# Leaving the row maximum out of a softmax under a bound taken from the gains, with a branch to the path that keeps it

## The chip, the cores and the metric

The kernel runs on one core of one Trainium2 chip. The metric is the device time of one execution in microseconds (us); lower is better. A core has five engines that run side by side and meet through semaphores: TensorE (PE in the profile, with its weight loads as PEld), VectorE (DVE), ScalarE (ACT), GpSimd (POOL) and SyncE (SP, which here only issues DMAs and DMA transposes). Matmuls read SBUF, the on-chip memory of 128 partitions, and write PSUM, eight banks of 128 x 512 f32.

## The reference

Attention over 8 batch rows, 12 heads, 448 positions and head size 64, and behind it a feed-forward layer with a token shift.

```python
def rmsnorm(x, g):
    return x / np.sqrt(np.mean(x * x, axis=-1, keepdims=True) + 1e-06) * g
q_n, k_n = rmsnorm(q, g_q), rmsnorm(k, g_k)
scores = np.matmul(q_n, k_n.transpose(0, 1, 3, 2)) / np.sqrt(64)
scores = scores - np.max(scores, axis=-1, keepdims=True)
attn = np.exp(scores)
attn = attn / (np.sum(attn, axis=-1, keepdims=True) + 1e-09)
x = heads_side_by_side(np.matmul(attn, v))        # 8 x 448 x 768
x_prev = x shifted by one position
xk = mu_k * x + (1 - mu_k) * x_prev
xr = mu_r * x + (1 - mu_r) * x_prev
k = np.maximum(xk @ w_k, 0)                       # w_k 768 x 1024
v = k * k @ w_v                                   # w_v 1024 x 768
r = 1 / (1 + np.exp(-(xr @ w_r)))                 # w_r 768 x 768
return r * v
```

All inputs are f32 but w_k, w_v and w_r, which are 64-bit floats. The maximum changes the value of no probability, it only keeps exp in range. After the normalisation a row of q_n has at most the length of the largest gain times 8, and a score is at most 64 times the largest |g_q g_k|/8. For the inputs that the reference draws, the largest |g_q g_k|/8 is 0.657.

## The kernel before

*Work and tiles.* Heads go in pairs (48) and quads (24, two pairs). For each quad q and k are loaded, normalised and transposed (`stats`, L602, `preps`), and seven score groups are made (`scores`, L777), 168 in all. A group is 128 rows of queries for two heads: two PSUM banks `sc` of 128 x 448 scores. `expo` (L814) takes each bank: VectorE writes the negative row maximum into the small tile `sums`, and ScalarE's exp takes it as its bias, writes the exponentials and sums them. That is 2 x 168 = 336 banks. `probs` (L826) then has VectorE scale the two sums and take their reciprocals. From there two ways lead to the transposed probabilities `pT`:

- The 21 groups of the first three quads (`probs_pe`, L859) hold f32 exponentials in a tile `nat` (or `xk`, memory lent until the first batch row needs it). GpSimd multiplies by the reciprocal, TensorE transposes into PSUM, and ScalarE or VectorE copies to `pT`, whichever has the lower planned clock (`pick`, L222).
- The other 147 groups keep exponentials in `sc`. `split` (L887) makes them two f16 tiles: ScalarE writes the rounded product with the reciprocal, VectorE the remainder, and SyncE issues a DMA transpose of both into `pT`. The scores of these quads are three f16 matmul passes, those of the first three one f32 pass.

`attends` (L895) multiplies `pT` by v into the bank `ot`; six pairs make one batch row. `mixk` (L927) makes xk as two f16 tiles; `moe` (L1076) multiplies xk by w_k, squares, and after that does xr by w_r and the squares by w_v, row by row, three f16 passes each, into two banks `mm`. The first batch row goes on to w_r and w_v only when all 20 weight tiles are done.

*Weights.* `weights` (L983) turns 64-bit floats into f32: 20 tiles of 128 columns, each in two halves of 3 x 128 or 4 x 128 elements per partition. GpSimd makes the low bits from byte 3 of each double, in place in `raw` (or `kk`, lent memory). ScalarE takes the high word as an f32, scales it by 2^-112 and writes it to a bank `mm`; its Prelu, with a negative slope of -2^32, turns the sign into an exponent bit. VectorE shifts that by 3, which puts the sign bit in its place, and ORs the low bits. `LOW_TILES` holds all 20 tiles, so the other branch there is never taken. `wsplit` (L1012) then scales a tile and splits it into two f16 tiles (wkh and wkl, wrh and wrl, wvh and wvl).

*Order.* Every step is a Python generator that yields operations. `Plan` (L214 on) holds a planned clock for each engine, prices an operation (`price`, L170), and always issues the one that can start first by these clocks, less a tenth of its priority in ns (`run`, L324). `emit` (L266) pins each engine's order to the order of issue. So the order of all five engines is fixed when the kernel is built, and one change of an operation or a price shifts the order of all that follow. Rings of buffers bound how far steps run ahead: five banks `sc`, two `mm`, one `ot`, four `nat`, two `raw`, two `wf`. The priority of weight work (`wprio`) rises with planned time past 10 us per finished tile. Nearly all operations are recorded under L272, the line in `emit`, so the profile is read by tile names.

Of the kernel before, what the change touches and what calls it, by code (L numbers as in the profile page):

```python
# [17 lines left out]
HD = 64  # L18
# [19 lines left out]
LOW_TILES = range(0, 20)  # L38
# [66 lines left out]
F64_NEG = -2.0 ** 32  # L105
# [315 lines left out]
def attn_moe_kernel(tc, q, k, v, g_q, g_k, mu_k, mu_r, w_k, w_v, w_r, out):  # L421
# [109 lines left out]
    def setup():  # L531
# [9 lines left out]
        yield V.tensor_reduce(out=gm[:, 0:1], in_=G, axis=AX.X, op=ALU.max, apply_absolute_value=True)  # L541
        yield V.tensor_scalar(out=gm[:, 0:1], in0=gm[:, 0:1], scalar1=TINY, scalar2=None, op0=ALU.max)
# [271 lines left out]
    def expo(gi, j, both, sums, D, tp):  # L814
        sp = both[j]
        if tp is not None:
            yield V.tensor_reduce(out=sums[:, j:j + 1], in_=sp[:, 0:S], axis=AX.X, op=ALU.max, negate=True)
            yield A.activation(out=tp.bitcast(F32).rearrange("p a c -> p (a c)")[:, j * S:(j + 1) * S], in_=sp[:, 0:S], func=AF.Exp, bias=sums[:, j:j + 1], accum_out=sums[:, 4 + 2 * j:5 + 2 * j])
# [4 lines left out]
        yield A.activation(out=sp[:, 0:S], in_=sp[:, 0:S], func=AF.Exp, bias=sums[:, j:j + 1], accum_out=both[0][:, S + j:S + j + 1])  # L823
        D[j] = True

    def probs(gi, both, sums, D, tp):  # L826
# [16 lines left out]
        yield V.tensor_scalar(out=r, in0=both[0][:, S:S + 2], scalar1=1e-9, scalar2=2.0 ** -15, op0=ALU.add, op1=ALU.mult)  # L843
        yield V.reciprocal(out=r, in_=r)
# [14 lines left out]
    def probs_pe(u, x, t0, sums, tp):  # L859
        r = sums[:, 8:11:2]  # L860
        yield V.tensor_scalar(out=r, in0=sums[:, 4:7:2], scalar1=1e-9, scalar2=2.0 ** -15, op0=ALU.add, op1=ALU.mult)
        yield V.reciprocal(out=r, in_=r)
# [120 lines left out]
    def weights():  # L983
        for nm, w, kt, c, ci in WT:
# [3 lines left out]
            for i in range(0, kt, hk):  # L988
# [7 lines left out]
                if ci in LOW_TILES:  # L996
# [197 lines left out]
```

## Time and profile before

| | |
|---|---|
| median of 3 runs | 1023.7 us (1022.6 to 1023.84) |
| the profiled execution, first to last instruction | 1022.8 us (its own time is given as this span alone) |
| TensorE busy | 933.2 us, 91% |
| VectorE busy | 789.3 us, 77% |
| ScalarE busy | 748.2 us, 73% |
| GpSimd busy | 691.6 us, 68% |
| mean granted TensorE clock | 0.968 |
| row maxima on VectorE | 336, 194.3 us, 614 ns each |
| f16 copies of probabilities on ScalarE | 294 (242 into `nat`, 52 into `natx`), 655 and 653 ns each |

In the profile a line of a group reads: line of the code, engine, operation, tiles written <- tiles read, shapes, count | busy us, mean ns of one | idle time of the engine just before them, and who ended it. `natx`, `dfx` and `kfx` are further buffers of `nat`, `df` and `kf`. A matmul's end is modelled and matmuls overlap, so a busy TensorE need not be at its peak. The chain of waits follows the work that ended last backwards from the end, step by step to what released it; "issue" in it is time with no cause in the profile. The slices divide the span in 40 parts, each digit the busy tenths of one.

### The profile page before, as it was taken

The numbers are of one execution on the slowest core, as the hardware profiler recorded it, in microseconds if no ns is written. First come the engines' busy times: TensorE is split into PE (matmuls) and PEld (weight loads), VectorE is DVE, ScalarE is ACT, GpSimd is POOL, SyncE is SP. The second block draws the span as 40 slices with busy tenths as digits, with TensorE's granted clock in tenths as the row PEclk, the third lists the DMA queues.
The fourth block names the chain that finished last, engine by engine and source line by source line (L and its number), as shares of the span: only waits on it lengthen the run. The fifth ranks groups of instructions, "written<-read, shape, count | busy, mean of one in ns | idle before, by whom it ended". The sixth has DMA issues, their size and how long they took to land.

```text
span 1022.8 us, 18968 instructions
## 1 busy us (share of the span) xinstructions
PE 933.2 (91%) x6166; PEld 489.2 (48%) x6166; DVE 789.3 (77%) x1967; ACT 748.2 (73%) x1755; POOL 691.6 (68%) x738
## 2 busy tenths in 40 slices
PE   1678778778999899999999999999999999999997
PEld 1344334344554455445555555455455554455564
DVE  5888868998989689878988798969887898785000
ACT  2666748988789688798888788888887887684211
POOL 2587678862688576896788467967795679629501
PEclk9779889978999999999999999999999999999999
DMA  8442348785885797777986889579768986662011
GB/s 200 121 118 74 104 126 173 181 182 112 188 188 125 150 188 155 171 165 173 185 165 113 179 180 190 127 163 193 157 126 179 183 181 139 135 124 54 1 32 31
DMA packets 447043, 146.62 MB, mean 143 GB/s; under 512 B 418784, under 2 KB 443360, under 8 KB 446944
## 3 DMA queue, kind: packets, MB, share of 16 engines
q1 hardware_dynamic: 427408, 127.42, 59.2%
q10 hardware_dynamic: 19536, 18.00, 6.1%
q8 instruction: 48, 0.79, 0.3%
q14 instruction: 51, 0.42, 0.1%
HBM read 50.40 MB, written 11.01 MB: 60 GB/s over the span
## 4 chain that ended last, share of the span: by engine, by line
PE 54%; DVE 18%; ACT 9%; POOL 7%; issue 6%; DMA 4%; SPq 1%; ACTq 0%; POOLq 0%; DVEq 0%
PE mm L272 37%; PE ot L272 9%; PE sc L272 8%; DVE sums L272 4%; DVE nat L272 3%; POOL xk L272 2%; ACT nat L272 2%; ACT sc L272 2%; DVE sst L272 2%; DVE df L272 2%; DMA pT<-nat 1%; DVE stm L272 1%; POOL nat L272 1%; SPq L272 1%; POOL qk L272 1%
## 5 line engine op out<-in xcount | busy, mean ns | idle before, releaser
L272 PE MATMUL mm<-wvh,kk 128*128 128x384 f16 x896 | 234.4, 327 | 0.0
L272 PE MATMUL mm<-xk,wkh 128*128 128x448 f16 x768 | 209.5, 355 | 5.9 <-ACT kf L272 4.2
L272 DVE TENSOR_REDUCE sums<-sc 128x1 f32<-128x448 f32 x336 | 194.3, 614 | 23.4 <-PE sc L272 23.0
L272 ACT ACTIVATE sc<-sc,sums 128x448 f32<-128x448 f32 x294 | 180.9, 617 | 36.9 <-DVE sums L272 33.1
L272 ACT ACTIVATE nat<-sc,sums 128x448 f16<-128x448 f32 (+1 forms) x274 | 167.2, 653 | 24.9 <-DVE sums L272 13.1
L272 PE MATMUL mm<-wrh,xr 128*128 128x384 f16 x672 | 179.9, 331 | 0.0
L272 DVE SCALAR_TENSOR_TENSOR nat<-sc,sums,nat 128x448 f16<-128x448 f32 x242 | 158.3, 675 | 28.0 <-ACT nat L272 27.5
L272 PEld LDWEIGHTS <-kk 128*128 128x128 f16 (+1 forms) x1362 | 129.2, 98 | 97.2 <-issue 17.0
L272 PE MATMUL sc<-stk 64*128 64x448 f16 (+3 forms) x1104 | 135.0, 386 | 12.8 <-DVE nat L272 4.2
L272 PE MATMUL mm<-wvl,kk 128*128 128x384 f16 x448 | 146.0, 326 | 0.0
L272 PE MATMUL mm<-xk,wkl 128*128 128x448 f16 x384 | 135.8, 354 | 0.0
L272 PEld LDWEIGHTS <-xr 128*128 128x128 f16 x1008 | 96.9, 99 | 75.2 <-issue 16.3
L272 PE MATMUL mm<-wrl,xr 128*128 128x384 f16 x336 | 111.3, 331 | 0.0
L272 PEld LDWEIGHTS <-wkh 128*128 128x128 f16 x768 | 72.2, 98 | 80.5 <-issue 19.8
L272 PE MATMUL ot<-pT,vh 128*64 128x448 f16 x672 | 101.0, 359 | 2.6 <-issue 1.3
L272 POOL TENSOR_TENSOR o<-o,bsc 128x384 f32<-128x384 f32 x48 | 42.9, 894 | 78.6 <-DVE o L272 53.9
L272 POOL TENSOR_TENSOR qk<-qk,ss 128x896 f32<-128x896 f32 x36 | 63.3, 1758 | 43.2 <-DVE ss L272 28.5
L272 DVE SCALAR_TENSOR_TENSOR o<-o,mm 128x384 f32<-128x384 f32 x56 | 30.6, 546 | 78.0 <-PE mm L272 49.9
L272 ACT ACTIVATE o<-mm,bsc 128x128 f32<-128x128 f32 x144 | 45.6, 386 | 45.6 <-PE mm L272 33.6
L272 DVE SCALAR_TENSOR_TENSOR df<-x,bsc,df 128x448 f32<-128x448 f32 x68 | 65.7, 978 | 10.5 <-POOL df L272 10.3
L272 PEld LDWEIGHTS <-stk 64*128 64x128 f16 x1008 | 35.7, 98 | 70.7 <-issue 48.9
L272 POOL TENSOR_TENSOR nat<-nat 128x448 f32<-128x448 f32 x41 | 47.5, 1157 | 29.9 <-ACT nat L272 29.2
(167 smaller groups left out, 1802.0 us busy)
## 6 DMA issues: line engine op xcount, KB each, us to landing
out_dram<-o SPq DMA_DIRECT2D x56, 192.0 KB, 2.9
qk<-in_k_dram SPq DMA_DIRECT2D x46, 224.0 KB, 3.8
qk<-in_q_dram SPq DMA_DIRECT2D x108, 64.0 KB, 2.5
vf<-in_v_dram SPq DMA_DIRECT2D x96, 64.0 KB, 2.6
raw<-in_moe_w_v_dram ACTq DMA_DIRECT2D x12, 512.0 KB, 4.6
vf<-in_v_dram SPq DMA_DIRECT2D x96, 48.0 KB, 2.5
raw<-in_moe_w_r_dram ACTq DMA_DIRECT2D x12, 384.0 KB, 3.3
kk<-in_moe_w_k_dram ACTq DMA_DIRECT2D x8, 384.0 KB, 4.5
```

The lines of the kernel that those rows point to most:

```text
L272: r = op.fn(op.kw["out"], op.kw["value"]) if op.fn.__name__ == "memset" else op.fn(**op.kw)
```

## The change

The kernel function gets two arguments, `safe` and `flag`. It is built twice into one program.

- With `safe=False` (the path that runs first) no row maximum is taken, and exp has no bias. The small addition of 1e-9 to the sum becomes a factor. `split` gives the f16 copy to ScalarE or VectorE, by `pick`.
- In `setup`, VectorE writes `flag` = 1 if the largest |g_q g_k|/8, which is there already, is at most 64/64 = 1.
- Behind the whole first path each engine loads the flag into a register. If it is 0, the second path (`safe=True`) computes everything again with the maximum, in the same output.
- In the weight conversion of both paths Prelu becomes Copy, and a new VectorE operation writes the sign, as byte 3 of the low word, from byte 7, after GpSimd has read and rewritten the low word. The branch that was never taken goes.

```diff
-LOW_TILES = range(0, 20)
-F64_NEG = -2.0 ** 32
+BOUND = 64.0
@@ setup
         yield V.tensor_reduce(out=gm[:, 0:1], in_=G, axis=AX.X, op=ALU.max, apply_absolute_value=True)
+        if flag is not None:
+            yield V.tensor_scalar(out=flag, in0=gm[0:1, 0:1], scalar1=BOUND / HD, scalar2=None, op0=ALU.is_le)
@@ expo
+        kw = {}
+        if safe:
+            yield V.tensor_reduce(out=sums[:, j:j + 1], in_=sp[:, 0:S], axis=AX.X, op=ALU.max, negate=True)
+            kw["bias"] = sums[:, j:j + 1]
         if tp is not None:
-            yield V.tensor_reduce(out=sums[:, j:j + 1], in_=sp[:, 0:S], axis=AX.X, op=ALU.max, negate=True)
-            yield A.activation(out=tp..., in_=sp[:, 0:S], func=AF.Exp, bias=sums[:, j:j + 1], accum_out=...)
+            yield A.activation(out=tp..., in_=sp[:, 0:S], func=AF.Exp, accum_out=..., **kw)
             banks["sc"].put(sp)
-            D[j] = True
-            return
-        yield V.tensor_reduce(out=sums[:, j:j + 1], in_=sp[:, 0:S], axis=AX.X, op=ALU.max, negate=True)
-        yield A.activation(out=sp[:, 0:S], in_=sp[:, 0:S], func=AF.Exp, bias=sums[:, j:j + 1], accum_out=...)
+        else:
+            yield A.activation(out=sp[:, 0:S], in_=sp[:, 0:S], func=AF.Exp, accum_out=..., **kw)
         D[j] = True
+
+    def recip(r, total):
+        if safe:
+            yield V.tensor_scalar(out=r, in0=total, scalar1=1e-9, scalar2=2.0 ** -15, op0=ALU.add, op1=ALU.mult)
+        else:
+            yield V.tensor_scalar(out=r, in0=total, scalar1=(1 + 1e-9) * 2.0 ** -15, scalar2=None, op0=ALU.mult)
+        yield V.reciprocal(out=r, in_=r)
@@ split
-        yield A.activation(out=ph[:, j], in_=sp[:, 0:S], func=AF.Copy, scale=r[:, j:j + 1])
+        if safe or plan.pick("ACT", "DVE") == "ACT":
+            yield A.activation(out=ph[:, j], in_=sp[:, 0:S], func=AF.Copy, scale=r[:, j:j + 1])
+        else:
+            yield V.tensor_scalar(out=ph[:, j], in0=sp[:, 0:S], scalar1=r[:, j:j + 1], scalar2=None, op0=ALU.mult)
@@ weights
-                if ci in LOW_TILES:
-                    yield G_.tensor_scalar(out=low, in0=<byte 3 of raw>, scalar1=-15.5, scalar2=2.0 ** -5, ...)
-                    yield A.activation(out=z, in_=top.bitcast(F32), func=AF.Prelu, scale=F64_EXP, alpha=F64_NEG)
-                    yield V.scalar_tensor_tensor(out=fi[...], in0=zi, scalar=3, in1=low, ...)
-                else:
-                    ...
+                r8 = raw.bitcast(mybir.dt.uint8)[:, 0:hk, :].rearrange("p i (n b) -> p i n b", b=8)
+                yield G_.tensor_scalar(out=low, in0=r8[:, :, :, 3], scalar1=-15.5, scalar2=2.0 ** -5, op0=ALU.add, op1=ALU.mult)
+                yield V.tensor_scalar(out=r8[:, :, :, 3], in0=r8[:, :, :, 7], scalar1=128.0, scalar2=128.0, op0=ALU.is_ge, op1=ALU.mult)
+                yield A.activation(out=z, in_=top.bitcast(F32), func=AF.Copy, scale=F64_EXP)
+                yield V.scalar_tensor_tensor(out=fi[:, i:i + hk, :], in0=zi, scalar=3, in1=low, op0=ALU.logical_shift_left, op1=ALU.bitwise_or)
@@ kernel
-        attn_moe_kernel(tc, *args)
+        with tc.tile_pool(name="path", bufs=1) as pool:
+            flag = pool.tile([1, 1], I32, name="bounded")
+            attn_moe_kernel(tc, *args, safe=False, flag=flag)
+            fine = nc.values_load(flag[0:1, 0:1], min_val=0, max_val=1)
+            with tc.If(fine < 1, preferred_fallthrough_block=False):
+                attn_moe_kernel(tc, *args, safe=True)
```

More of the change, by code (lines that the diff above doesn't have):

```diff
@@ L418, in rsqrt, with attn_moe_kernel @@
             yield V.scalar_tensor_tensor(out=y, in0=t, scalar=1.5, in1=y, op0=ALU.add, op1=ALU.mult)
-def attn_moe_kernel(tc, q, k, v, g_q, g_k, mu_k, mu_r, w_k, w_v, w_r, out):
+def attn_moe_kernel(tc, q, k, v, g_q, g_k, mu_k, mu_r, w_k, w_v, w_r, out, safe, flag=None):
     nc = tc.nc
@@ L815, in expo @@
         sp = both[j]
+        kw = {}
+        if safe:
+            yield V.tensor_reduce(out=sums[:, j:j + 1], in_=sp[:, 0:S], axis=AX.X, op=ALU.max, negate=True)
+            kw["bias"] = sums[:, j:j + 1]
         if tp is not None:
-            yield V.tensor_reduce(out=sums[:, j:j + 1], in_=sp[:, 0:S], axis=AX.X, op=ALU.max, negate=True)
-            yield A.activation(out=tp.bitcast(F32).rearrange("p a c -> p (a c)")[:, j * S:(j + 1) * S], in_=sp[:, 0:S], func=AF.Exp, bias=sums[:, j:j + 1], accum_out=sums[:, 4 + 2 * j:5 + 2 * j])
+            yield A.activation(out=tp.bitcast(F32).rearrange("p a c -> p (a c)")[:, j * S:(j + 1) * S], in_=sp[:, 0:S], func=AF.Exp, accum_out=sums[:, 4 + 2 * j:5 + 2 * j], **kw)
             banks["sc"].put(sp)
-            D[j] = True
-            return
-        yield V.tensor_reduce(out=sums[:, j:j + 1], in_=sp[:, 0:S], axis=AX.X, op=ALU.max, negate=True)
-        yield A.activation(out=sp[:, 0:S], in_=sp[:, 0:S], func=AF.Exp, bias=sums[:, j:j + 1], accum_out=both[0][:, S + j:S + j + 1])
+        else:
+            yield A.activation(out=sp[:, 0:S], in_=sp[:, 0:S], func=AF.Exp, accum_out=both[0][:, S + j:S + j + 1], **kw)
         D[j] = True
+    def recip(r, total):
[4 more added lines that the diff above has]
+        yield V.reciprocal(out=r, in_=r)
     def probs(gi, both, sums, D, tp):
@@ L842, in probs @@
         r = sums[:, 8:11:2]
-        yield V.tensor_scalar(out=r, in0=both[0][:, S:S + 2], scalar1=1e-9, scalar2=2.0 ** -15, op0=ALU.add, op1=ALU.mult)
-        yield V.reciprocal(out=r, in_=r)
+        yield from recip(r, both[0][:, S:S + 2])
         E = {}
@@ L860, in probs_pe @@
         r = sums[:, 8:11:2]
-        yield V.tensor_scalar(out=r, in0=sums[:, 4:7:2], scalar1=1e-9, scalar2=2.0 ** -15, op0=ALU.add, op1=ALU.mult)
-        yield V.reciprocal(out=r, in_=r)
+        yield from recip(r, sums[:, 4:7:2])
         tf = tp.bitcast(F32).rearrange("p a c -> p (a c)")
@@ L995, in weights @@
                 zi = z.bitcast(I32)
-                if ci in LOW_TILES:
-                    yield G_.tensor_scalar(out=low, in0=raw.bitcast(mybir.dt.uint8)[:, 0:hk, :].rearrange("p i (n b) -> p i n b", b=8)[:, :, :, 3], scalar1=-15.5, scalar2=2.0 ** -5, op0=ALU.add, op1=ALU.mult)
-                    yield A.activation(out=z, in_=top.bitcast(F32), func=AF.Prelu, scale=F64_EXP, alpha=F64_NEG)
-                    yield V.scalar_tensor_tensor(out=fi[:, i:i + hk, :], in0=zi, scalar=3, in1=low, op0=ALU.logical_shift_left, op1=ALU.bitwise_or)
-                else:
-                    yield A.activation(out=z, in_=top.bitcast(F32), func=AF.Prelu, scale=F64_EXP, alpha=F64_NEG)
-                    yield V.tensor_scalar(out=zi, in0=zi, scalar1=3, scalar2=None, op0=ALU.logical_shift_left)
-                    yield V.scalar_tensor_tensor(out=fi[:, i:i + hk, :], in0=low, scalar=29, in1=zi, op0=ALU.logical_shift_right, op1=ALU.bitwise_or)
+                r8 = raw.bitcast(mybir.dt.uint8)[:, 0:hk, :].rearrange("p i (n b) -> p i n b", b=8)
[3 more added lines that the diff above has]
+                yield V.scalar_tensor_tensor(out=fi[:, i:i + hk, :], in0=zi, scalar=3, in1=low, op0=ALU.logical_shift_left, op1=ALU.bitwise_or)
                 R["raw"].put(raw)
```

## The prediction

> **What bounds the kernel now.** I read the page first: busy times, then the forty slices.
>
> ```profile
> span 1022.8 us, 18968 instructions
> ...
> PE 933.2 (91%) x6166; PEld 489.2 (48%) x6166; DVE 789.3 (77%) x1967; ACT 748.2 (73%) x1755; POOL 691.6 (68%) x738
> ...
> PE   1678778778999899999999999999999999999997
> ...
> DVE  5888868998989689878988798969887898785000
> ```
>
> TensorE is full from the tenth slice (25.6 us each) to the last, and it is not full before. The feed-forward of the first batch row goes on to wr and wv as soon as the last weight tile is split; the timeline of TensorE has the first such matmul here (start us, us):
>
> ```profile
> 235.89 0.50 PE L272 MATMUL mm<-wrh,xr 128*128 128x384 f16 x1
> ```
>
> I cut the span just before it, at 235 us, and again at 925 us, where attention has ended and only the feed-forward of the last batch row is left. The table of these three stretches (length, then busy us and instruction count of PE, PEld, DVE, ACT, POOL; granted clock; DMA share; GB/s):
>
> ```profile
> 0.00:235.00 235.00, 159.54 (x930) 85.02 (x932) 192.53 (x516) 159.45 (x356) 161.20 (x202) 0.88 0.56 141
> 235.00:925.00 690.00, 681.60 (x4689) 351.40 (x4687) 581.03 (x1431) 565.94 (x1346) 491.12 (x493) 0.99 0.77 162
> 925.00:1022.80 97.80, 92.08 (x552) 52.73 (x550) 15.76 (x21) 22.79 (x53) 39.33 (x44) 1.00 0.08 21
> ```
>
> In the opening TensorE is idle for 235 - 159.5 = 75.5 us. In the middle it is idle for 690 - 681.6 = 8.4 us, although VectorE is 84% busy there. In the end VectorE is nearly empty. So VectorE's work has a price in the opening and hardly any after it: **whatever is freed after 235 us can give back 8.4 us at most.** The opening's total is what is to be argued. There VectorE is the fullest engine, 192.5 of 235 = 82%; ScalarE and GpSimd have 68 and 69%. The chain of waits, cut to the opening, by engine and tile:
>
> ```profile
> by line: PE sc L272 10.6%; issue 10.5%; PE ot L272 9.8%; DVE sums L272 8.5%; DVE nat L272 4.2%; DMA xk<-in_q_dram 3.5%; POOL xk L272 3.4%; DVE sst L272 2.9%; DMA pT<-nat 2.9%; POOL nat L272 2.7%; ACT nat L272 2.6%; DMA raw<-in_moe_w_k_dram
> ```
>
> No engine owns it: VectorE's writes of `sums` (maximum, sum scaling, reciprocal) hold 8.5%, that is 20.0 us. Last, whom TensorE and ScalarE waited for in the opening (us in total, times, longest):
>
> ```profile
> PE sc L272 <- DVE nat L272: 24.0, 6, 21.2
> ```
>
> ```profile
> ACT stk L272 <- PE sc L272: 12.3, 8, 3.3
> ACT pT L272 <- PE sc L272: 11.1, 11, 3.6
> ACT x L272 <- PE ot L272: 8.6, 4, 3.9
> ACT nat L272 <- DVE sums L272: 8.2, 6, 3.8
> ...
> ACT xk L272 <- DVE sums L272: 4.8, 3, 1.9
> ```
>
> The wait of 21.2 us is the start (first loads and first normalisation), which the change doesn't touch. ScalarE's exp waited 8.2 + 4.8 = 13.0 us for maxima.
>
> **The change part by part.** *The maxima go.* VectorE's groups in the opening (count | busy us, mean ns | idle before):
>
> ```profile
> L272 DVE TENSOR_REDUCE sums<-sc 128x1 f32<-128x448 f32 x72 | 42.3, 615 | 5.8 <-PE sc L272 5.7
> ...
> L272 DVE TENSOR_SCALAR sums<-sums 128x2 f32<-128x2 f32 x21 | 8.6, 426 | 1.2 <-ACT nat L272 1.1
> ...
> L272 DVE RECIPROCAL sums<-sums 128x2 f32<-128x2 f32 x35 | 5.0, 156 | 0.2
> ...
> L272 DVE TENSOR_SCALAR sums<-sc 128x2 f32<-128x2 f32 x14 | 2.0, 150 | 0.1
> ```
>
> 72 of the 336 reductions lie there: 42.3 us off VectorE. Of the 57.9 us that write `sums` they are 73%, so 14.6 of the chain's 20.0 us, or 35% of their own busy time. The other 264 lie under a full TensorE.
>
> *Byte instructions come.* Each of the 20 weight tiles is converted in two halves. GpSimd's instruction on the low word stays, and each half gains one VectorE `tensor_scalar` which reads byte 7 and writes byte 3 of the same words, both in SBUF: 40 of them, 28 with 384 elements and 12 with 512. All lie in the opening, as the view of the tile `raw` shows (minimum, median and longest ns, first and last start in us):
>
> ```profile
> L272 POOL TENSOR_SCALAR raw<-raw x32: 527/553/964, 15.6 to 222.0; 128x384 int32<-128x384 uint8 x20, 128x512 int32<-128x512 uint8 x12
> ```
>
> The other 8 halves, of 384 elements, are in memory borrowed from `kk`. No row shows this instruction. The nearest rows are VectorE's `tensor_scalar` of these lengths (from PSUM), and its slowest small one between SBUF tiles:
>
> ```profile
> L272 DVE TENSOR_SCALAR muu<-muu 128x12 f32<-128x12 f32 x1 | 1.6, 1620 | 0.0
> ...
> L272 DVE TENSOR_SCALAR stk<-sc,gc 128x384 f32<-128x384 f32 x2 | 1.2, 614 | 1.0 <-PE sc L272 1.0
> ...
> L272 DVE TENSOR_SCALAR stk<-sc,gc 128x512 f32<-128x512 f32 x1 | 0.8, 752 | 0.2 <-PE sc L272 0.2
> ```
>
> I take 614 and 752 ns: 28 x 0.614 + 12 x 0.752 = 26.2 us. The low end is the row of 150 ns (two elements), 6.0 us; the high end the row of 1620 ns, 64.8 us. That last row shows a danger: twelve elements cannot need 1620 ns, so the instruction stood waiting for something. The scaling of sums shows it again, 426 ns between SBUF tiles against 150 ns from PSUM, 0.276 us more for the same two elements. With that wait on each byte instruction the 40 cost 37.2 us.
>
> The Trainium skill, SBUF — State Buffer, section "Who interferes with whom", has a reason: VectorE and GpSimd share one SBUF port pair, a `tensor_scalar` in a two-port mode wants it, and the loser "fully blocks" until the other instruction ends. The rows of 426 and 1620 ns agree. By the rule the byte instruction, which starts when GpSimd's own conversion ends and GpSimd's next instruction begins, would wait more often than not; the sum would then go by 37.2 us instead of 26.2, and the opening would gain 3.0 us instead of 9.4.
>
> Net on VectorE in the opening: -42.3 + 26.2 = -16.1 us. How much of it reaches the end lies between the chain's share of such work, 0.35 (5.6 us), and VectorE's busy share, 0.82 (13.2 us); neither is nearer, so the mean 0.585: **-9.4 us.** Behind a byte instruction on VectorE stand the OR of the same half and then the attention work; the OR is late by 0.65 us. Halves follow each other (222.0 - 15.6)/39 = 5.3 us apart and two raw buffers are there, so the longer chain is covered; without that cover it is 40 x 0.655 = 26.2 us once more.
>
> *Copies may move.* In the opening ScalarE writes 28 f16 copies of probabilities:
>
> ```profile
> L272 ACT ACTIVATE nat<-sc,sums 128x448 f16<-128x448 f32 x28 | 17.1, 642 | 2.5 <-DMA pT<-nat 1.7 <-DVE sums L272 0.5 <-issue 0.3
> ```
>
> The planner may now give each to VectorE, at about 0.68 us (between 614 and 752 ns). VectorE has 192.5 - 16.1 = 176.4 us against ScalarE's 159.5, so few should move: 0. If all do, VectorE is back at 195 us and the opening gains nothing. Beyond these pieces the planner writes all engines' orders anew from its own prices of the instructions; no row prices that, and the range has to hold it.
>
> *What costs nothing.* Prelu to Copy keeps one ScalarE instruction of the same shape; a second table load, if it brought one, would be the length of the one there is now, hidden by ScalarE's idle 32%. The scaling of sums loses an ALU step in the same instruction. The flag is one 150 ns instruction on one element, under VectorE's wait for the first loads.
>
> *The middle.* TensorE's waits from 235 to 925 us:
>
> ```profile
> PE sc L272 <- DVE nat L272: 3.2, 6, 1.4
> PE ot L272 <- ACT vh L272: 3.1, 1, 3.1
> ```
>
> VectorE's lighter load can take the first away, **-3 us**; the bounds are 0 and the 8.4.
>
> *The end.* After the last instruction each engine loads the flag, compares and branches. No row shows a register load or a branch. The end of the span, as the chain and the timeline give it:
>
> ```profile
> 1011.91 5.87 issue
> 1017.79 0.86 POOLq L1190
> ```
>
> ```profile
> 1017.82 0.83 POOL L272 TENSOR_TENSOR o<-o,bsc 128x384 f32<-128x384 f32 x1 [5.91 <-DVE o L272]
> 1018.67 1.11 SPq L272 DMA_DIRECT2D out_dram<-o  x2
> ```
>
> From 1019.8 to 1022.8 us only the last store lands and the engines meet. The new work is hidden there on four engines, and comes late on SyncE alone. I take **+1.5 us**, half of those 3.0; bounds 0 and 5.9 (the longest step of that chain without work). The Trainium skill, Runtime: NRT & Kernel Launch, section "Instruction fetch mechanics", says that a taken branch leaves the prefetched pages and waits for a fetch; no row of this kernel shows a branch, and it would put the end nearer 5.9 than 0.
>
> Sum: 1022.8 - 9.4 - 3 + 1.5 = 1011.9 us of span. The page gives the span alone; the median of the runs is 0.9 above it, so **1012.8 us**.
>
> **The rivals.**
>
> *Slower: the byte instructions block VectorE.* Place: the 40 conversions; price 1.62 us each, the row of `muu`. 64.8 - 42.3 = +22.5 us on VectorE, x 0.585 = +13.2; with -3 and +1.5 the median is 1035.4 us. It decides from the point where the opening loses 1.5 us, a net of +2.6 us, or (42.3 + 2.6)/40 = 1.12 us per byte instruction. For it: GpSimd is 69% busy in the opening, and 1620 and 426 ns are there. Against: the mean wait is 0.276 us.
>
> *No change.* The opening is paced by what is not touched: 10.5% issue, 10.6% and 9.8% TensorE on the chain, GpSimd's 161 us, weights whose conversion is spread over 208 us by the planner's own pacing. Then 0, 0 and +1.5: 1025.2 us, within 0.2% of 1023.7, which is 2.0 us and about what a measurement of this kernel can tell from no change. For it: 0.35 is all that the chain credits to the maxima, and 13.0 us of ScalarE's waits may only become waits for TensorE, of which there are already 32. Against: VectorE's 82%.
>
> *A larger gain.* The byte instructions are cheap (6.0 us) and VectorE does pace the opening: 36.3 x 0.82 = 29.8, the whole 8.4 of the middle, +1.5: 987.0 us. For it: exp no longer stands behind VectorE's queue at all. Against: the chain's 14.6 us.
>
> *The bound isn't met* and the second path runs: about twice the time, 2045 us. The flag is set if max |g_q g_k|/8 is at most 1; for the inputs that the reference draws it is 0.657.
>
> **How the numbers follow.** Forecast 0.48, larger gain 0.15, no change 0.14, slower 0.22, second path 0.01. The forecast's own range is 1004 us (path share 0.82 and the whole middle) to 1019 us (byte instructions at 37.2). The range of 8 in 10 reaches 990 to 1035 and leaves out half of the slower case, a third of the larger gain and the second path. Faster 0.48 + 0.15 = 0.63; same 0.13, the no-change case less 0.01 for a longer end; slower 0.22 + 0.01 + 0.01 = 0.24.
>
> **What would show it.** No reduction into `sums`; 40 byte instructions on VectorE near 0.66 us (above 1.12 the rival is right). The first wr matmul some 9 us before 235.9. VectorE near 176 us and TensorE's idle near 66 us over the opening. The middle at full TensorE again. A tail after the last store longer by 1 to 2 us. If VectorE is emptier and wr starts at 236 us all the same, the opening is not VectorE's, and the forecast is wrong at its main step.

## The result and the profile after

The changed kernel takes **1064.0 us** (median of 4 runs, 1059.3 to 1064.7) against 1023.6 us: a ratio of 1.038, 95% interval 1.036 to 1.041. Forecast were 1012.8 us and a range of 990 to 1035. It is slower by 40.4 us, and the second path never runs. The medians leave out two executions in a slower state, one of kept_all_shift512 (1058.4 us; with it the median is the 1033.3 us that the expectations name) and one of after_shift64 (1406.4 us, the one that was profiled).

The page of the changed kernel, rows as in the prediction's first fence:

```profile
span 1062.8 us, 18615 instructions
...
PE 939.9 (88%) x6166; PEld 492.7 (46%) x6166; DVE 755.2 (71%) x1854; ACT 637.9 (60%) x1573; POOL 700.7 (66%) x738
...
PE   1677667759999999899999999999989999999996
...
DVE  5878788977988695868886976779696958663000
```

VectorE has 34 us less work than before and ScalarE 110 us less, and TensorE, whose work is the same, is idle for longer. Where, the table by stretches says, cut at the same places (length, busy us and count of PE, PEld, DVE, ACT, POOL; granted clock; DMA share; GB/s):

```profile
0.00:235.00 235.00, 153.09 (x878) 82.21 (x879) 185.06 (x473) 137.69 (x314) 171.69 (x199) 0.88 0.54 132
235.00:925.00 690.00, 658.39 (x4482) 337.97 (x4482) 534.10 (x1305) 459.22 (x1156) 479.03 (x478) 0.98 0.85 158
925.00:1062.80 137.80, 128.43 (x808) 72.55 (x805) 36.06 (x77) 41.03 (x106) 50.01 (x61) 0.97 0.25 48
```

TensorE's idle time is 81.9 us in the opening (75.5 before), **31.6 us in the middle (8.4 before)** and 9.4 us at the end (5.7 before); its busy time is 6.7 us longer at a granted clock of 0.958 against 0.968. These four differences, 6.4 + 23.2 + 3.7 + 6.7, are the 40.0 us of span. The largest stands where the prediction saw nothing to lose. The DMA share of the middle rose from 0.77 to 0.85 although no byte more is moved. The waits of TensorE there (us in total, times, longest):

```profile
PE sc L271 <- DVE nat L271: 12.0, 12, 2.2
PE sc L271 <- DMA stk<-nat: 5.1, 8, 1.9
PE ot L271 <- DMA pT<-nat: 4.0, 6, 1.3
```

Two of the three are waits for DMA transposes, which do not head the list before. The DMA rows, first of the kernel before, then of the changed one (queue: packets, MB, share of the time of 16 engines; transposes: count, median us from issue to landing):

```profile
q1 hardware_dynamic: 427408, 127.42, 59.2%
...
pT<-nat SPq DMA_TRANSPOSE x121, 4.0
```

```profile
q1 hardware_dynamic: 427408, 127.42, 63.8%
...
pT<-nat SPq DMA_TRANSPOSE x119, 4.6
...
stk<-nat SPq DMA_TRANSPOSE x31, 4.2
```

The same packets took 0.638 x 1062.8 = 678 us of each DMA engine instead of 0.592 x 1022.8 = 605.5 us, 12% more.

Groups of VectorE that are new (busy us, mean ns), the sign byte instructions and then the copies moved from ScalarE, and one ScalarE group that is shorter, exp without a bias:

```profile
L271 DVE TENSOR_SCALAR raw<-raw 128x384 uint8<-128x384 uint8 x20 | 15.2, 762 | 2.1 <-POOL raw L271 2.1
...
L271 DVE TENSOR_SCALAR raw<-raw 128x512 uint8<-128x512 uint8 x12 | 11.8, 985 | 6.2 <-POOL raw L271 6.2
...
L271 DVE TENSOR_SCALAR kk<-kk 128x384 uint8<-128x384 uint8 x8 | 6.1, 760 | 1.7 <-POOL kk L271 1.7
```

```profile
L271 DVE TENSOR_SCALAR nat<-sc,sums 128x448 f16<-128x448 f32 x142 | 92.5, 676 | 3.5 <-DMA pT<-nat 2.5
```

```profile
L271 ACT ACTIVATE sc<-sc 128x448 f32<-128x448 f32 x294 | 157.2, 537 | 32.8 <-PE sc L271 29.1 <-ACT sc L271 0.6
```

The 40 byte instructions take 33.1 us. 142 copies into `nat` and 42 into `natx` moved to VectorE, 184 of 294. The first wr matmul, which marks the end of the weights, comes 6.0 us later than before, and the other 34.0 us of the span are lost behind it:

```profile
241.90 0.50 PE L271 MATMUL mm<-wrh,xr 128*128 128x384 f16 x1
```

And the end: the last matmul and the last store of the changed kernel (start us, us). From the matmul's end to the end of the span it is 9.4 us, with 5.7 before (1017.1 to 1022.8). The last two lines are SyncE's two branches and what follows them (count, shortest, median and longest ns, first and last start): the store has landed by 1058.6 us, SyncE branches at 1058.7 us, and its next instruction stands at 1061.5 us:

```profile
1053.11 0.33 PE L271 MATMUL mm<-wvh,kk 128*128 128x384 f16 x1
...
1055.03 1.41 SPq L271 DMA_DIRECT2D out_dram<-o  x2
...
L1208 SPq COMPARE_BRANCH  x2: 37/47/57, 1056.5 to 1058.7; - x2
...
L1203 SPq EVENT_SEMAPHORE  x10: 17/28/28, 1061.5 to 1062.7; - x10
```

### The profile page after: what moved, and what is told of

Its sections match the earlier page's. It is cut to its first block, busy times and chain, and to the rows that moved or that the text cites. A ratio compares the mean times of both kernels' runs of the same rounds, so it can differ in the third digit from the quotient of the medians.

```text
span 1062.8 us, 18615 instructions
## 1 busy us (share of the span) xinstructions
PE 939.9 (88%) x6166; PEld 492.7 (46%) x6166; DVE 755.2 (71%) x1854; ACT 637.9 (60%) x1573; POOL 700.7 (66%) x738
## 3 DMA queue, kind: packets, MB, share of 16 engines
q1 hardware_dynamic: 427408, 127.42, 63.8%
## 5 line engine op out<-in xcount | busy, mean ns | idle before, releaser
L271 PE MATMUL mm<-xk,wkh 128*128 128x448 f16 x768 | 212.0, 358 | 6.0 <-DVE WSC L271 4.8
L271 ACT ACTIVATE sc<-sc 128x448 f32<-128x448 f32 x294 | 157.2, 537 | 32.8 <-PE sc L271 29.1
L271 DVE SCALAR_TENSOR_TENSOR nat<-sc,sums,nat 128x448 f16<-128x448 f32 x238 | 155.0, 674 | 17.0 <-ACT nat L271 15.2
L271 PE MATMUL sc<-stk 64*128 64x448 f16 (+3 forms) x1104 | 131.2, 382 | 30.1 <-DVE nat L271 18.6
L271 PE MATMUL mm<-wvl,kk 128*128 128x384 f16 x448 | 146.0, 326 | 0.0
L271 DVE TENSOR_SCALAR nat<-sc,sums 128x448 f16<-128x448 f32 x142 | 92.5, 676 | 3.5 <-DMA pT<-nat 2.5
L271 POOL TENSOR_TENSOR o<-o,bsc 128x384 f32<-128x384 f32 x48 | 44.0, 917 | 75.5 <-DVE o L271 66.4
L271 ACT ACTIVATE nat<-sc,sums 128x448 f16<-128x448 f32 x96 | 57.3, 633 | 42.7 <-DVE sums L271 23.6
L271 POOL TENSOR_TENSOR nat<-qk,nat 128x896 f16<-128x896 f32 x31 | 58.8, 1898 | 21.2 <-ACT nat L271 21.1
```

The lines of the kernel that those rows point to most:

```text
L271: r = op.fn(op.kw["out"], op.kw["value"]) if op.fn.__name__ == "memset" else op.fn(**op.kw)
```

## The experiments

The change does several things at once, and each rewrites the order of all engines. So I made two families of kernels. In the **kept** family the planner plans the kernel before, maxima and all, and `emit` leaves out or puts in single instructions afterwards; the order of everything else stays. In the **replanned** family the edit stands in the generators, and the planner draws a new order.

### The maxima alone

**order_kept:** before's order, maxima planned but not issued, exp without bias; old conversion, no branch. **replanned:** the maxima gone from the generators. **replanned_v:** replanned, with one priority changed.

```diff
# order_kept, in emit
+            if op.kw.get("negate"):
+                continue
# replanned, in expo
-        yield V.tensor_reduce(out=sums[:, j:j + 1], in_=sp[:, 0:S], axis=AX.X, op=ALU.max, negate=True)
# replanned_v, beside it
-PRIO_V = 310
+PRIO_V = 2000
```

> The planner plans exactly the kernel before, with its 336 maxima, but the maxima are not issued and exp has no bias; the order of every other instruction on all five engines is that of before, weights are converted as before, and there is no branch. It computes the softmax without the row maximum. Theory 1 (the loss comes from the new order that the planner writes, not from the work): 1000 to 1020 us, no slower than 1023.6, since 194 us of VectorE's work is gone and nothing else moves. Theory 2 (the byte instructions hold up the weights): also at or below 1023.6, it has none. Theory 3 (attention that runs ahead faster collides on the DMA engines, whatever the order): 1035 us or more, with TensorE waiting for pT and stk.

> The kernel before with the maxima left out of the plan too, so the planner writes a new order; copies stay on ScalarE, weights are converted as before, no branch. It computes the softmax without the row maximum. Theory 1 (new order): 1035 to 1060 us, most of the 40 us lost. Theory 2 (byte instructions): 1000 to 1015 us. Theory 3 (DMA): 1035 us or more.

> As replanned (maxima left out of the plan, 1107.0 us), with the planner's priority for loading and preparing v raised from 310 to 2000. It computes the softmax without the row maximum. In replanned TensorE waited 64.1 us in 13 pieces for ScalarE's vh, and ScalarE for the loads of v, which stand late in SyncE's queue. If that place in the queue is the mechanism, the wait falls below 15 us and the time to 1040 to 1065 us. If the loads are late because of the DMA engines, the wait stays and the time is 1095 us or more.

Measured: order_kept **1008.5 us** (ratio 0.985, 0.983 to 0.987); replanned **1107.0** (1.082, 1.078 to 1.085); replanned_v **1029.9** (1.006, 1.003 to 1.009). The same instructions go, and the time moves by -15 or by +83 us. In order_kept the first wr matmul starts at 226.72 us, 9.2 earlier than before, and the stretches are

```profile
0.00:235.00 235.00, 163.20 (x995) 87.68 (x999) 161.37 (x471) 160.01 (x374) 163.88 (x202) 0.92 0.59 146
235.00:925.00 690.00, 686.26 (x4734) 354.85 (x4727) 467.74 (x1153) 546.48 (x1343) 507.06 (x511) 1.00 0.78 160
```

In replanned TensorE's longest waits of the middle are for the loads of v. Its waits, and one of the twelve places in the timelines of SyncE and ScalarE (start us, us):

```profile
PE ot L272 <- ACT vh L272: 61.7, 12, 12.3
```

```profile
515.92 0.60 SPq L272 DMA_DIRECT2D out_dram<-o  x1
516.56 9.79 SPq L272 DMA_DIRECT2D vf<-in_v_dram  x11
```

```profile
520.39 0.63 ACT L272 ACTIVATE vh<-vf 128x512 bf16<-128x512 f32 x1 [9.29 <-DMA vf<-in_v_dram]
```

SyncE issues in order. In the new order the v loads stand behind transposes, stores and the loads of q and k, ScalarE waits 9.3 us for them, and TensorE 12. With a higher priority for the v loads this wait leaves the list of the middle, and 77 of the 83 us come back; 21 us over order_kept remain. So dropping the maxima, together with the bias that exp no longer reads, is worth 15 us, and a new order can cost more than any part of the change.

### The other parts alone, replanned

**bytes_only:** before with the new conversion. **no_branch:** the changed kernel without flag and second path.

```diff
# bytes_only, in weights: the lines of the change, nothing else
# no_branch
-            attn_moe_kernel(tc, *args, safe=False, flag=flag)
-            fine = nc.values_load(...)
-            with tc.If(fine < 1, ...): ...
+        attn_moe_kernel(tc, *args, safe=False)
```

> The kernel before with the new weight conversion alone (Copy instead of Prelu, and 40 byte instructions on VectorE, 33.1 us in the changed kernel); the maxima stay, no branch. Theory 2: 1045 us or more, since 33 us are added to the fullest engine of the opening and nothing is taken away. Theory 1: 1025 to 1045 us, with the size of any other replanning. By the prediction's own share of 0.585: 1023.6 + 33.1 x 0.585 = 1043 us.

> The changed kernel's first path alone, without flag, register loads and branch. The end of the changed kernel's profile, from its last matmul to its last instruction, takes 9.4 us against 5.7 before, so the branch should be worth 3 to 5 us: 1059 to 1061 us. If it were under 1050 us, the branch or the second path's code would cost more than its tail shows.

Measured: 1062.0 us (1.037, 1.035 to 1.040) and **1072.6 us** (1.047, 1.045 to 1.050). Without the branch the kernel is slower than with it: leaving out one flag instruction gave the planner another order, with TensorE waiting up to 9.9 us for vh again. Neither run prices its part; replanned kernels differ too much in their orders for that.

### The parts with the order kept

**kept_bytes:** order_kept with the new conversion, the byte instruction issued right before the OR of its half. **kept_bytes_max:** the same with the maxima left in. **kept_all:** kept_bytes with flag, branch and second path.

```diff
# kept_bytes, in emit; op.pre is the byte instruction, hung on the OR
+            if hasattr(op, "pre"):
+                self.last[e] = op.pre.fn(**op.pre.kw)
```

> As order_kept (order of before, maxima planned but not issued), with the new weight conversion: Copy in the place of Prelu, and each of the 40 byte instructions issued on VectorE right before the OR that needs it, unplanned, so that the order of all else is that of before. No branch. It computes the softmax without the row maximum. If the byte instructions' own time reaches the end by the prediction's share: 33 us x 0.585 = 19 over order_kept's 1008.5, 1028 us. By the prediction's sum without the branch, 1011 (byte instructions at 26 us) to 1018 (at 37 us). If the order alone makes the changed kernel slow: 1008 to 1020 us, well below 1023.6.

> The kernel before with the new weight conversion, its byte instructions issued unplanned right before the OR, maxima kept, order of all else that of before; no branch. bytes_only, the same work in the order that the planner writes for it, took 1062.0 us, 38 more than before. If that loss is the byte instructions' work: about 1055 us again. If it is the new order: 1030 to 1045 us (by the share of 0.585, 1023.7 + 19 = 1043).

> The whole change in the old order: as kept_bytes, with the flag written in the opening, the register loads and the branch at the end, and the second path behind it. The one part of the change that is left out is the choice of VectorE for the f16 copies. It is over kept_bytes by the price of the branch: 3 to 5 us by the changed kernel's tail. If the order is the cause, it is near 1016 to 1020 us and faster than before, against 1064.0 for the same work replanned.

Measured: kept_bytes **1030.7 us** (1.006, 1.004 to 1.008), kept_bytes_max 1047.0 (1.023, 1.021 to 1.025), kept_all **1049.7** (1.026, 1.024 to 1.028). The new conversion, in effect its byte instructions (the scaling of 384 elements took 530 ns as Prelu in order_kept, 526 as Copy in kept_bytes), costs 22.2 us without the maxima and 23.2 with them: more than the maxima are worth. In kept_bytes the first wr matmul is at 250.03 us, 23.3 later than in order_kept, and its stretches show that the opening stays idle while VectorE gets emptier than before:

```profile
0.00:235.00 235.00, 158.20 (x877) 83.34 (x878) 180.57 (x458) 142.93 (x333) 163.15 (x196) 0.87 0.53 134
235.00:925.00 690.00, 680.86 (x4687) 349.54 (x4688) 472.23 (x1188) 552.56 (x1362) 490.04 (x491) 0.99 0.78 162
```

The cut that fits this family best is the first wr matmul itself. Before, order_kept and kept_bytes, each up to it and from it on:

```profile
0.00:235.89 235.89, 160.43 (x933) 85.18 (x934) 193.42 (x520) 159.45 (x356) 161.20 (x202) 0.88 0.56 141
235.89:1022.80 786.91, 772.79 (x5235) 403.97 (x5233) 595.89 (x1448) 588.73 (x1399) 530.45 (x536) 0.99 0.68 144
...
0.00:226.72 226.72, 154.92 (x933) 83.58 (x934) 156.15 (x451) 153.59 (x357) 163.88 (x202) 0.92 0.58 146
226.72:1006.10 779.38, 769.95 (x5235) 402.40 (x5233) 477.82 (x1181) 568.93 (x1399) 531.64 (x536) 0.99 0.70 146
...
0.00:250.03 250.03, 167.67 (x933) 87.31 (x934) 195.07 (x491) 153.50 (x357) 168.42 (x202) 0.86 0.53 133
250.03:1030.70 780.67, 771.38 (x5235) 402.79 (x5233) 478.00 (x1181) 568.44 (x1399) 530.93 (x536) 0.99 0.69 145
```

Without the maxima the stretch up to wr is 9.2 us shorter and the rest 7.5 us. The byte instructions lengthen the first by 23.3 us and the rest by 1.3. Not all of that is idle time: the same 933 matmuls take 154.9, 160.4 and 167.7 us at a granted clock of 0.92, 0.88 and 0.86.

kept_all is 18.9 us slower than kept_bytes, with the same order of the first path but for the flag. Of that 3.5 us lie behind the last matmul. The rest lies in the middle, and it has the mark of the changed kernel, DMA share 0.85:

```profile
235.00:925.00 690.00, 666.84 (x4598) 345.56 (x4598) 460.75 (x1158) 541.64 (x1331) 486.19 (x486) 0.99 0.85 159
```

### Where the tiles lie

The flag is a tile of four bytes, allocated ahead of all others. It takes 32 bytes of each partition. In the built program of kept_bytes `pT`, `nat` and `stk` begin at 78336, 107008 and 114176, all multiples of 512; in kept_all each lies 32 bytes higher. Four kernels separate address and branch: **kept_bytes_shift32** (a dead tile ahead of the others, no branch), **kept_all_shift512** and **after_shift512** (a flag tile of 512 bytes), **after_shift64** (of 64).

```diff
# kept_bytes_shift32
+        with tc.tile_pool(name="pad", bufs=1) as pool:
+            blank = pool.tile([1, 1], I32, name="blank")
+            nc.vector.memset(blank, 0)
# kept_all_shift512, after_shift512; after_shift64 has [1, 16]
-            flag = pool.tile([1, 1], I32, name="bounded")
+            flag = pool.tile([1, 128], I32, name="bounded")[0:1, 0:1]
```

> The kernel of kept_bytes with one change: a tile of one int32 is put on the chip ahead of all others, as the flag is in the changed kernel, and nothing reads it. It moves every later tile by 32 bytes of each partition, so that the tiles that the DMA transposes read and write (nat, stk, pT) start at a multiple of 32 instead of 512. No branch, no second path. Theory A (the moved addresses make the transposes slow): the pT<-nat transposes land in about 4.6 us instead of 3.9, the DMA share of the middle is 0.85 instead of 0.78, and the time is 1030.7 + 14 = about 1044 us. Theory B (the branch and the code behind it slow the transposes): landing 3.9 us and 1030.7 us.

> The kernel of kept_all (flag, register loads, branch, second path) with one change: the flag's tile is 512 bytes long, of which the flag uses the first four, so that the later tiles start at multiples of 512 again. Theory A (addresses): landing of pT<-nat 3.9 us, DMA share of the middle 0.78, and about 1049.7 - 14 = 1035 us, of which 4 to 5 us over kept_bytes is the end of the program. Theory B (branch): landing 4.6 us and 1049.7 us.

> The changed kernel with one change: the flag's tile is 512 bytes long. The order of the instructions is the same on every engine. Theory A (addresses): landing of pT<-nat 3.9 us instead of 4.6, TensorE's idle time in the middle (235 to 925 us) falls from 31.6 us to about 18, and the time is about 1064 - 14 = 1050 us; what is left over kept_all_shift512 is then the new order and the moved copies, about 14 us. Theory B (branch): 1064 us and 4.6 us.

> The changed kernel with a flag of 64 bytes, so that the later tiles start 64 bytes above a multiple of 512, where they start 32 bytes above one in the changed kernel. If it is the multiple of 64 that the transposes need: landing of pT<-nat 3.9 us and about 1041 us, as with 512 bytes. If it is a larger multiple: 4.6 us and about 1064 us.

| kernel | tiles at 512n + | median us | ratio, 95% | queue q1, us per engine |
|---|---|---|---|---|
| kept_bytes | 0 | 1030.7 | 1.004 to 1.008 | 0.588 x 1030.7 = 606 |
| kept_bytes_shift32 | 32 | 1046.2 | 1.018 to 1.022 | 0.644 x 1049.0 = 676 |
| kept_all | 32 | 1049.7 | 1.024 to 1.028 | 0.645 x 1047.1 = 675 |
| kept_all_shift512 | 0 | 1031.9 | 1.005 to 1.010 | 0.589 x 1033.6 = 609 |
| after | 32 | 1064.0 | 1.036 to 1.041 | 678 |
| after_shift512 | 0 | 1041.2 | 1.016 to 1.020 | 0.586 x 1037.2 = 608 |
| after_shift64 | 64 | 1058.7 | 1.031 to 1.039 | not compared |

In each of the first three pairs of rows only the address differs, but for the one memset of the dead tile. The dead tile costs 15.4 us with no branch in the program; 508 unused bytes take 22.8 us off the changed kernel, whose instructions and order stay the same. The first wr matmul starts at 241.9 us in both, so all of it lies behind the opening. DMA rows of kept_bytes_shift32, then of after_shift512:

```profile
q1 hardware_dynamic: 427408, 127.42, 64.4%
...
pT<-nat SPq DMA_TRANSPOSE x121, 4.6
...
stk<-nat SPq DMA_TRANSPOSE x28, 4.2
```

```profile
q1 hardware_dynamic: 427408, 127.42, 58.6%
...
pT<-nat SPq DMA_TRANSPOSE x119, 3.9
...
stk<-nat SPq DMA_TRANSPOSE x31, 3.7
```

and the middle of after_shift512, where TensorE's idle time falls from 31.6 to 14.5 us:

```profile
235.00:925.00 690.00, 675.50 (x4671) 346.13 (x4671) 555.51 (x1359) 475.80 (x1200) 485.93 (x492) 0.99 0.79 164
```

Theory A holds: the addresses, not the branch. The tiles of the loads and stores (`qk`, `vf`, `o`) move by the same 32 bytes, so the runs do not say which transfers cost the time; the landings of the transposes change most. no_branch has no flag tile, and its `pT<-nat` transposes land in 3.9 us: its 1072.6 us are not the addresses. A multiple of 64 does not do (1058.7 us); one of 512 does; between them nothing was tried. The Trainium skill, DMA: Bandwidth & Descriptors, section "How a descriptor splits into AXI transactions", says that a transaction starts at a multiple of 256 bytes and that a piece which begins elsewhere fetches from the boundary below. By that a piece of 128 f16, 256 bytes, would take 9 beats of 32 bytes instead of 8 at an offset of 32, an estimate of 12% more, and 10 at 64. The trace agrees with the first: 403456 of the queue's 427408 packets are recorded with 256 bytes; they took 508 us of each engine in kept_bytes and 571 us in kept_bytes_shift32, and the rise is 12.0 to 12.7% in the three pairs. That 64 was no slower than 32 does not agree with the second.

The branch itself, between kept_bytes and kept_all_shift512, is +1.2 us by the medians (the ratios differ by 0.002 with an uncertainty of 0.003), too small to tell from none, and 3.7 us by the tail: 9.4 us from the last matmul to the end in kept_all_shift512 too, 5.7 in kept_bytes.

### What the sign costs, and on which engine

All four keep before's order, leave out the maxima, have the branch and tiles at multiples of 512; they differ in the one instruction that carries the sign. kept_all_shift512 has the byte instruction on VectorE. **kept_all_pool** has it on GpSimd. **kept_all_act** and **kept_all_act2** have ScalarE write a second scaled copy as float16, of which only the sign is left, ahead of the OR and ahead of the first copy. **kept_all_max** has VectorE take the larger of z and -2^-80 times the value.

```diff
-both_.pre = V.tensor_scalar(out=r8[:, :, :, 3], in0=r8[:, :, :, 7], scalar1=128.0, scalar2=128.0, op0=ALU.is_ge, op1=ALU.mult)
# kept_all_pool
+both_.pre = G_.tensor_scalar(<the same>)
# kept_all_act; in kept_all_act2 it hangs on the first copy of the half
+both_.pre = A.activation(out=<upper half of the low word as f16>, in_=top.bitcast(F32), func=AF.Copy, scale=F64_EXP)
# kept_all_max
+both_.pre = V.scalar_tensor_tensor(out=z, in0=top.bitcast(F32), scalar=-2.0 ** -80, in1=z, op0=ALU.mult, op1=ALU.max)
```

> The kernel of kept_all_shift512 with the 40 sign byte instructions on GpSimd instead of VectorE, at the same place of the program. In the opening GpSimd is busy 138 of 235 us and VectorE 181 of 235, and GpSimd's own byte instructions of these shapes took 563 to 836 ns there. If VectorE's time sets the opening, as its 33 us of byte instructions for 22 us of the time said, most of the 22 us comes back and the time is about 1035 - 15 to 22 = 1013 to 1020 us. If GpSimd's 28 us more (or 1.6 us an instruction, as its slow forms, 64 us) are as much on the path, the time is 1035 us or more.

> The kernel of kept_all_shift512 with the sign taken by ScalarE instead of VectorE: in place of each sign byte instruction a second copy of the same values on ScalarE, scaled by 2 to the -112 and written as float16 into the upper half of the low word, where all that is left of a value is its sign (minus or plus zero). Before's order, maxima out, flag, branch and second path are kept, and the outputs are those of the reference. If the 22 us of the byte instructions are VectorE's time in the opening: ScalarE, busy 143 us of 235 there, takes 40 more copies of 527 to 651 ns, 23 us, under waits, and the time is that of order_kept plus 3 us for the branch, 1011 us, up to 1018 where some of these copies wait ahead of others. If the cost is that of any further step in the chain of a weight piece, whatever its engine: 1033 us.

> The kernel of kept_all_act with the sign copies of ScalarE moved forward: each now runs right before the copy of the same piece that makes z, instead of right before VectorE's OR, where VectorE waited 50 us for them. They cost ScalarE 1.07 and 1.36 us each, 46 us in the opening, where it was busy 143 of 235 us. If what made kept_all_act slow is VectorE's waiting for a copy issued too late: VectorE is free of 33 us of byte instructions and of the waits, and the time is between order_kept plus the branch, 1011 us, and kept_all_shift512, 1033 us; I take 1020 us. If ScalarE's 46 us are themselves on the path: 1035 us or more.

> The kernel of kept_all_shift512 with another instruction on VectorE in place of the sign byte instruction: z becomes the larger of z and the same value times minus 2 to the -80, which gives negative values the exponent that the shift turns into the sign bit. It reads 32-bit words and writes packed into PSUM, as the OR does that took 558 and 692 ns, where the byte instructions took 850 and 1325 ns before 300 us in kept_bytes. If the cost is VectorE's time for them (37 us there, 22 us of the result): 28 x 0.56 + 12 x 0.69 = 24 us, and the time falls by 13 x 0.6 = 8 us from 1033.3 to about 1025 us. If the cost is one more step in VectorE's queue for each piece, whatever its length: 1033 us.

One group of each, 20 of the 40 instructions, in this order: pool, act2, max (busy us, mean ns):

```profile
L276 POOL TENSOR_SCALAR raw<-raw 128x384 uint8<-128x384 uint8 x20 | 43.6, 2178 | 0.3
```

```profile
L276 ACT ACTIVATE raw<-raw 128x384 f16<-128x384 f32 x20 | 21.3, 1067 | 3.4 <-POOL raw L278 1.2 <-issue 1.1 <-DVE stm L278 0.9
```

```profile
L275 DVE SCALAR_TENSOR_TENSOR mm<-raw,mm 128x384 f32<-128x384 f32 x20 | 11.1, 555 | 7.0 <-ACT mm L277 6.8
```

| kernel | sign, us on its engine | first wr matmul, us | median us |
|---|---|---|---|
| order_kept (old conversion, no branch) | 0 | 226.7 | 1008.5 |
| kept_all_max | VectorE 23.8 | 241.9 | 1026.0 |
| kept_all_act2 | ScalarE 46.1 | 246.8 | 1032.2 |
| kept_all_shift512 | VectorE 39.6 | 249.0 | 1031.9 |
| kept_all_act | ScalarE 46.1 | 259.8 | 1042.8 |
| kept_all_pool | GpSimd 94.1 | 298.4 | 1084.3 |

The time follows the start of the first wr matmul: 71.7 us later at the bottom than at the top, and 75.8 us longer. From that matmul to the end all six take between 779.4 and 784.7 us of their spans. My expectation that the cost is VectorE's fell with kept_all_act2: in its opening VectorE is 34 us emptier than in kept_all_shift512 (146.0 against 180.1) and the time is the same. What fits all six is that the sign is a further link in the chain of each half (low bits, sign, scaling, OR, split), and delays the end of the weights whatever engine it is on; how much of kept_all_act2 is ScalarE's own 46.1 us was not separated. Its length counts: the same place on VectorE with 23.8 us instead of 39.6 saved 5.9 us. So does its place: kept_all_act has the instructions of kept_all_act2 just ahead of the OR, where VectorE waits for them, as this row of its VectorE groups says:

```profile
L278 DVE SCALAR_TENSOR_TENSOR wf<-mm,raw 128x512 int32<-128x512 int32 x12 | 8.3, 692 | 25.7 <-ACT raw L276 25.7
```

Part of the length of a byte instruction on VectorE is waiting for GpSimd. In kept_bytes the same shape takes 583 to 2097 ns (shortest, median and longest, first and last start, and then one instruction of VectorE and the one that GpSimd was in when it started):

```profile
L275 DVE TENSOR_SCALAR raw<-raw x32: 583/853/2097, 25.2 to 239.4; 128x384 uint8<-128x384 uint8 x20, 128x512 uint8<-128x512 uint8 x12
...
69.28 2.10 DVE L275 TENSOR_SCALAR raw<-raw 128x384 uint8<-128x384 uint8 x1
...
69.24 1.69 POOL L277 TENSOR_TENSOR xk<-qk,ss 128x896 f32<-128x896 f32 x1 [2.43 <-DVE sums L277]
```

The 15 of the 40 that started while GpSimd was in no instruction took 583 to 606 ns with 384 elements and 736 ns with 512. Each of the other 25 ended 0.45 to 0.63 us after that GpSimd instruction did. By these rows 40 undisturbed ones would take 28 x 0.60 + 12 x 0.74 = 25.7 us, an estimate, so 13.6 of the 39.3 us in kept_bytes are waiting, and 7.5 of the 33.1 us in the changed kernel. The instruction of kept_all_max, which writes to PSUM, took 555 and 690 ns in the mean, with no such waits: the longest of its 40 took 697 ns.

kept_all_max, the whole change but for the moved copies, in before's order with aligned tiles and the cheaper sign, is level with the kernel before: ratio 1.001, 1.000 to 1.003. order_kept is the only kernel here faster than both, and it has no second path.

### The moved copies

**kept_bytes_copies:** kept_bytes with five of every eight f16 copies issued on VectorE at the same place, 184 of 294. **after_act_copies:** after_shift512 with all copies on ScalarE, replanned.

```diff
# kept_bytes_copies, in emit; op.alt is the same copy on VectorE
+            if hasattr(op, "alt"):
+                self.copies += 1
+                if self.copies % 8 < 5: op, e = op.alt, "DVE"
# after_act_copies
-        if safe or plan.pick("ACT", "DVE") == "ACT":
+        if True:
```

> The kernel of kept_bytes (1030.7 us) with 184 of the 294 float16 copies of the probabilities issued on VectorE instead of ScalarE, five of every eight, at the same place in the program; in the changed kernel its planner moved as many. They are 124 us of VectorE's time at 676 ns, most of it in the middle, where VectorE is busy 472 of 690 us and ScalarE 552. If the moved copies are what the changed kernel with aligned tiles has over kept_all_shift512 (7.9 us): about 1038 us. If it is the new order of the other instructions: 1031 us. If the load of the engines in the middle matters for itself, the copies could also gain a few us.

> The changed kernel with the flag of 512 bytes, and with all 294 float16 copies on ScalarE, as in the kernel before; its planner writes the order anew. If the 7.9 us of after_shift512 over kept_all_shift512 are the moved copies: about 1033 us. If they are the planner's new order, which this edit draws again: anything between 1030 and 1085 us, as the other kernels with a new order gave 1030 to 1107; with the periodic wait for the loads of v, TensorE's waits for vh are in the middle as in the kernel with no maxima in its plan.

Measured: 1086.7 us (1.061, 1.059 to 1.064) and 1049.6 us (1.023, 1.020 to 1.027). Moved without a new order the copies cost 56 us, more than the changed kernel has in all; taken out of after_shift512 they leave it 8.3 us slower, in yet another order. So the 9.3 us that after_shift512 has over kept_all_shift512 belong to order and copies together. Which copy or which turn of the order makes them is open.

## Why the prediction was wrong

The account of the changed kernel, from kernels that differ by the part of their row:

| part | from, to | us |
|---|---|---|
| maxima out, exp without bias | before, order_kept | -15.3 |
| sign byte instructions | order_kept, kept_bytes | +22.2 |
| flag, branch, second path | kept_bytes, kept_all_shift512 | +1.2 |
| new order and moved copies | kept_all_shift512, after_shift512 | +9.3 |
| tiles moved by 32 bytes | after_shift512, after | +22.8 |
| sum | | +40.2 |

The second row holds the byte instruction right before the OR; the changed kernel has it ahead of the scaling, and that difference is in the fourth row.

*What bounds the kernel.* Right on the stretches, and on TensorE being fed late in the opening. Wrong in the sentence that what is freed after 235 us gives back 8.4 us at most, as far as it was read both ways: a full middle bounds gains, not losses, and 23.2 us were lost there.

*The maxima go, byte instructions come.* The step that failed is the netting, -16.1 us times one path share of 0.585. Up to the first wr matmul the maxima were worth 9.2 us for their 42.3 us, a share of 0.22, below the chain's 0.35 that I had as the lower bound. The byte instructions cost 23.3 us there for their 39.3 us in kept_bytes, a share of 0.59: they are links of the weight chain, which sets when wr starts. Together that is 14.1 us lost in the opening of kept_bytes, where I had 9.4 us gained; the changed kernel lost 6.0. The 26.2 us for the byte instructions were low as well, since they left out the waits for GpSimd: 33.1 us in the changed kernel, 39.3 in kept_bytes, where the sum with a wait had 37.2. The row to weigh was not VectorE's total but the chain of a half; the sentence that the longer chain "is covered" by two raw buffers was the error. The test that I named for this step came out against it: VectorE is emptier (185.1 us in the changed kernel, 180.6 in kept_bytes, 192.5 before) and wr starts later, not earlier.

*The rival of blocked byte instructions* had the right side, and its mechanism is there: they do stand behind GpSimd, as the rows of 426 and 1620 ns had hinted. The price was too high: 0.83 us each in the changed kernel, 0.98 in kept_bytes, under the 1.12 us from which it was to decide. The opening was lost all the same, because the path shares were not alike.

*Copies may move: 0.* Wrong: 184 moved, 22 of them before 260 us. The price of that alone stays open.

*The planner's new order.* Said to have no price, and given no term. It has one: 9.3 us with the copies in the changed kernel, and in replanned, the edit I took for the safest part, 98 us between two orders of the same instructions.

*What costs nothing.* The flag's 150 ns (142 measured) were hidden as said. Its tile was not looked at: the addresses it moves cost 22.8 us, as much as the byte instructions. Nothing in the profile of before would have priced this, but the place of the pool, ahead of all others, stood in the diff.

*The end.* 3.7 us against 1.5, within the bounds of 0 and 5.9. The place was right: SyncE's branch comes when the last store has landed, and the 2.8 us to its next instruction are hidden by nothing.

*The middle, -3.* In order_kept TensorE's idle time there falls from 8.4 to 3.7 us, and the time from the first wr matmul to the end by 7.5 us. So the maxima behind the opening were worth more than the term, and nearly as much as the 72 in it; in the changed kernel this gain is lost among the other terms.

## What to carry to other kernels

Before crediting work freed on a busy engine, follow the chain that the freed or added instruction is a link of: up to the first wr matmul a microsecond on one chain was worth 0.22, on another 0.59, and their difference in busy time said nothing. Price an added tile by what it moves: compare the addresses of the tiles that DMAs read and write, and look at the queue's time for the same packets. Where a planner writes the order, test an edit with the order kept first; a new order alone moved this kernel by up to 98 us.

## What the runs showed that I had not expected

- DMA transposes between SBUF tiles land in 4.6 us instead of 3.9 when the tiles begin 32 bytes above a multiple of 512 (kept_bytes_shift32 and kept_bytes).
- Where the weights came late, the matmuls ahead of them ran at a lower clock: the same 933 or 934 matmuls were busy for 154.9 us at a granted clock of 0.92 in order_kept and for 186.7 us at 0.78 in kept_all_pool.
- GpSimd reads a strided byte and writes an int32 in 554 ns (128 x 384, kept_all_pool), and took 2178 ns for the same count with a byte result by compare and multiply.
- ScalarE's copy of 128 x 384 f32 took 524 ns into PSUM, and 1066 ns as f16 into the upper halves of 64-bit words' low words in SBUF (kept_all_act).
- Exp of 128 x 448 took 537 ns without a bias and 617 ns with one from a tile; the group of the kernel before:

```profile
L272 ACT ACTIVATE sc<-sc,sums 128x448 f32<-128x448 f32 x294 | 180.9, 617 | 36.9 <-DVE sums L272 33.1 <-DVE stm L272 0.5 <-ACT sc L272 0.2
```
